# A Fourier mixer and a low-rank MLP: unfolded output weights without sums on GpSimd, and q stored by chunks of 256 tokens

## The chip, the cores and the metric

One core of one Trainium2 chip runs the whole program. The metric is the device time of one launch in microseconds (us). "Median" is over the timed runs of one kernel.

Engine names in profile lines: PE is TensorE (matmuls), PEld its weight loads, DVE is VectorE, ACT is ScalarE, POOL is GpSimd. "L425" is a line of that kernel's source; the line numbers of the two kernels differ by a few.

## The reference

```python
def _attn_ref(x):                        # x [8, 3136, 256] f32
    X = np.fft.fft(x, axis=1)
    X = np.fft.fft(X, axis=2)
    return X.real.astype(np.float32)

def _moe_ref(x, U, V, w_ch1, w_ch2):     # U [3136, 32], V [32, 3136], w_ch1 [256, 1024], w_ch2 [1024, 256]
    xt = x.transpose(0, 2, 1)
    h = xt @ U @ V
    u = x + h.transpose(0, 2, 1)
    ch = np.maximum(u @ w_ch1, 0.0) @ w_ch2
    return (u + ch).astype(np.float32)
# out = _moe_ref(_attn_ref(x), ...)      [8, 3136, 256] f32
```

The residual `u` is never built as a tensor: its two terms enter the output's accumulation as matmuls against small tables.

## The kernel before

The batch is worked in four pairs. In the steady part one step is made of two half-steps, and a half-step is one MLP1 unit (TensorE makes `hps`, ScalarE copies half of it to `ab`, VectorE makes two tiles `hT` out of both with `max`) and one MLP2 phase (16 matmuls of `hT` with `W2`, L480, and then the residual's matmuls against the tables `TK`, `Bp` and `R`, L490). In between, TensorE prepares the next pair: stage 1 (`s`, from the folded input `yb`), and then the transform's second stage (`ln`), which ScalarE copies into `q`, the tile that MLP1 and the residual read.

`W2` and `Bp` are folded: the 256 output columns are kept as 128 sums and 128 differences, so `Bp` is only 128 wide, and each output has to be put together again at the end, on GpSimd:

```python
def drain(eng):                                   # eng is nc.gpsimd but for the last chunk
    ...
    nc.scalar.copy(om, po)                        # ScalarE: PSUM -> SBUF
    eng.tensor_tensor(ob[:, 0:n, 0:P], a, om[:, :, 1], op=AL.add)
    eng.tensor_tensor(ob[:, 0:n, P:D], a, om[:, :, 1], op=AL.subtract)
```

The table part of a phase; each `o` is 256 columns, `half` says which 64 rows of the array the matmul uses, and matmuls on the two halves run side by side:

```python
def group(s, o, half):
    r = slice(64 * half, 64 * half + 64)
    if half == 0:
        yield o, VS[0:64, 1 - s, ...], TK[p2][b][:]
    for blk in range(2):
        w, cs = (RR[1 - s][r, blk], slice(0, D)) if half else (Bp[r, blk], slice(blk * P, (blk + 1) * P))
        yield o[:, cs], qs(r, s, blk), w
```

`q` is `[128, 2, 3200]`: two blocks of 128 columns of the model dimension, each with all tokens of the pair. One copy of 512 tokens writes a stretch in both blocks:

```python
o = q[:, :, c0:c0 + 512].rearrange("p k (i j s) -> p s k i j", i=4, s=2)
evac[0](o, ps[0].rearrange("p s (k i j) -> p s k i j", k=2, i=4))
```

VectorE also folds the next pair's input into `yb`, behind GpSimd's own fold into `y`:

```python
def fold_d(yb, src, l0, l1):
    nc.vector.tensor_tensor(o[:, :, 1:128], i[:, :, 1:128], i[:, :, 255:128:-1], op=AL.add)         # L143
    nc.vector.tensor_tensor(o[:, :, 129:256], i[:, :, 1:128], i[:, :, 255:128:-1], op=AL.subtract)  # L144
    nc.vector.tensor_copy(o[:, :, 0:129:128], i[:, :, 0:129:128])                                   # L145
```

## Time and profile before

| | before |
|---|---|
| time, median of 2 | 542.0 us (541.67 to 542.32) |
| span of the profiled run, mean granted TensorE clock | 543.4 us, 0.946 |
| TensorE from 45 us to the end | 425.2 us busy, 73.2 us idle |
| listed waits there: for q / for hT / for yb | 27.1 / 27.8 / 8.3 us |
| GpSimd busy | 271.4 us |
| the three instructions of the fold into yb, L143 / L144 / L145, mean of 24 | 1446 / 900 / 395 ns |

How to read it: time has to be looked for in TensorE's idle 73 us, and in what of its busy time is spent at the lower clock. The last two rows are not bounds by themselves.

### The profile page before, as it was taken

Reading aid. Unit: us, or ns where it says so; the run is one execution under the profiler, and the core shown is the slowest. Engines: PE = TensorE matmul, PEld = TensorE weight load, DVE = VectorE, ACT = ScalarE, POOL = GpSimd, SP = SyncE. Lnnn points to the kernel's source line nnn. Section 1 sums busy time; section 2 is a strip of 40 time slices with the busy share of each in tenths; the row PEclk is TensorE's granted clock in tenths of the full one; section 3 lists DMA queues with packets and bytes.
Section 4 is the critical chain, followed back from the end, with each engine's and each line's share of the span. In section 5 each row is a group of like instructions: output and inputs, shape, how many; then the busy total and the mean of one; then the engine's idle time right before and its main releaser. Section 6 shows DMA issues by size and latency. Waiting matters only on the chain.

```text
span 543.4 us, 18834 instructions
## 1 busy us (share of the span) xinstructions
PE 455.5 (84%) x8161; PEld 377.4 (69%) x8161; DVE 358.1 (66%) x613; ACT 291.5 (54%) x487; POOL 271.4 (50%) x372
## 2 busy tenths in 40 slices
PE   4886869897999789878888797987889889999996
PEld 2655757676778568757776576766667767888895
DVE  7645688766785456886786367686786355666673
ACT  4774544465644655654643655555454556656552
POOL 7358556467733446756552346574742313333341
PEclk9686998799999998999999999998899989999999
DMA  9436374348418434444515744454322911212122
GB/s 171 124 98 106 90 205 112 103 139 201 152 61 163 160 106 152 134 148 139 163 62 133 158 139 117 140 171 155 117 98 80 181 50 50 72 62 79 61 80 89
DMA packets 58339, 65.50 MB, mean 121 GB/s; under 512 B 11188, under 2 KB 51086, under 8 KB 58094
## 3 DMA queue, kind: packets, MB, share of 16 engines
q1 hardware_dynamic: 48048, 43.48, 27.9%
q0 software_dynamic: 7232, 14.30, 11.8%
q10 hardware_dynamic: 2976, 6.51, 3.2%
q8 instruction: 64, 1.05, 0.8%
q14 instruction: 19, 0.16, 0.1%
HBM read 34.62 MB, written 32.19 MB: 123 GB/s over the span
## 4 chain that ended last, share of the span: by engine, by line
PE 54%; DVE 26%; ACT 11%; issue 4%; DMA 2%; POOL 2%; ACTq 1%; DVEq 0%; POOLq 0%
PE ops L480 22%; PE hps L423 12%; DVE hT L441 7%; DVE hT L438 7%; PE hps L432 6%; PE ops L490 5%; ACT q L82 5%; DVE yb L143 4%; ACT ab L435 3%; DVE g L85 3%; DVE yb L144 2%; PE ln L355 2%; DMA w_f<-in_moe_w_ch_dram 1%; PE te L304 1%; PE teps L332 1%
## 5 line engine op out<-in xcount | busy, mean ns | idle before, releaser
L438 DVE SCALAR_TENSOR_TENSOR hT<-ab,hps 128x512 bf16<-128x512 bf16 x200 | 136.8, 684 | 167.1 <-ACT ab L435 164.8
L480 PE MATMUL ops<-W,hT 64*128 64x256 bf16 x3072 | 214.8, 277 | 13.0 <-DVE hT L441 8.5
L522 POOL TENSOR_TENSOR ob<-om 128x256 f32<-128x256 f32 (+1 forms) x97 | 71.5, 738 | 234.6 <-ACT om L521 225.4
L480 PEld LDWEIGHTS <-hT 64*128 64x128 bf16 x3072 | 158.4, 96 | 38.6 <-DVE hT L441 16.7
L435 ACT CAST ab<-hps 128x512 bf16<-128x512 f32 x200 | 117.1, 589 | 120.9 <-PE hps L432 115.1
L423 PE MATMUL hps<-q,W1p 64*128 64x256 bf16 (+1 forms) x1248 | 132.1, 276 | 41.7 <-ACT q L82 27.4
L441 DVE TENSOR_TENSOR hT<-hps,ab 128x512 bf16<-128x512 f32 x192 | 131.1, 683 | 0.0
L423 PEld LDWEIGHTS <-W1p 64*128 64x128 bf16 x1248 | 72.7, 97 | 58.9 <-issue 34.5
L423 PE MATMUL hps<-q,W1z 64*128 64x256 bf16 (+1 forms) x416 | 104.3, 276 | 0.0
L432 PE MATMUL hps<-VZ,TE 33*128 33x256 bf16 (+1 forms) x896 | 82.7, 267 | 0.6 <-ACT TE L82 0.6
L521 ACT COPY om<-ops 128x512 f32<-128x512 f32 (+1 forms) x97 | 56.4, 581 | 33.2 <-ACT q L82 10.1
L523 POOL TENSOR_TENSOR ob<-om 128x256 f32<-128x256 f32 (+1 forms) x97 | 73.6, 759 | 0.0
L153 POOL TENSOR_TENSOR y<-xa,xb 98x510 f32<-98x510 f32 (+1 forms) x48 | 58.1, 1229 | 2.4 <-DVE yb L145 2.4
L490 PE MATMUL ops<-TK,VS 64*128 64x256 f16 x192 | 52.8, 275 | 0.5 <-ACT TK L82 0.5
L432 PEld LDWEIGHTS <-TE 33*128 33x128 bf16 x896 | 44.7, 98 | 7.1 <-issue 1.6
L423 PEld LDWEIGHTS <-W1z 64*128 64x128 bf16 x416 | 40.3, 97 | 0.8 <-issue 0.4
L82 ACT CAST q<-ln 128x1024 bf16<-128x1024 f32 (+2 forms) x32 | 32.4, 1025 | 12.4 <-PE ln L355 11.9
L490 PEld LDWEIGHTS <-qr 64*128 64x128 bf16 x384 | 36.9, 96 | 2.4 <-issue 0.4
L490 PEld LDWEIGHTS <-q 64*128 64x128 bf16 x384 | 36.8, 96 | 2.4 <-issue 0.3
L490 PE MATMUL ops<-R,qr 64*128 64x256 f16 x192 | 38.0, 279 | 0.0
L82 ACT CAST z<-s 128x1024 bf16<-128x1024 f32 (+1 forms) x24 | 23.0, 959 | 27.6 <-PE s L196 25.8
L490 PE MATMUL ops<-R,q 64*128 64x256 f16 x192 | 36.6, 271 | 0.0
(186 smaller groups left out, 492.3 us busy)
## 6 DMA issues: line engine op xcount, KB each, us to landing
out_dram<-ob SPq DMA_DIRECT2D x192, 128.0 KB
xa<-in_x_dram SPq DMA_DIRECT2D x24, 392.0 KB
zturn<-z ACTq DMA_DIRECT2D x9, 512.0 KB
g<-zturn SPq DMA_DIRECT2D x6, 416.0 KB
g<-zturn SPq DMA_DIRECT2D x6, 384.0 KB
X<-in_x_dram POOLq DMA_DIRECT2D x4, 384.0 KB, 7.7
X<-in_x_dram POOLq DMA_DIRECT2D x2, 744.0 KB, 7.2
zturn<-z ACTq DMA_DIRECT2D x3, 448.0 KB
```

What stands on the lines that cost most here:

```text
L82: nc.scalar.copy(o, i)
L153: nc.gpsimd.tensor_tensor(ck.y[:, l0:l1, 1:256], ck.xa[:, l0:l1, 1:256], rb[:, l0:l1, 255:0:-1], op=AL.add)
L423: nc.tensor.matmul(o[s], lt, q[64 * s:64 * s + 64, blk, c0:c0 + w], start=(i == 0 and blk == 0), stop=True, skip_group_check=True)
L432: nc.tensor.matmul(ps[:, s, i * w + a:i * w + a + n], TE[ch.p % 2][b][64 * s:64 * s + 33, ja], VZ[64 * s:64 * s + 33, b, v:v + n], start=F ...
L435: nc.scalar.copy(ab[:], ps[:, 1])
L438: nc.vector.scalar_tensor_tensor(h[:, 1], b, -1.0, a, op0=AL.mult, op1=AL.max)
L441: nc.vector.tensor_tensor(flip[0][:, :, ::-1], flip[1], flip[2], op=AL.max)
L480: mm = nc.tensor.matmul(op, ch.h[rows[half], s, j, t * P:(t + 1) * P], W2[rows[half], j, :], start=(ha == 0 and j == 0), stop=False, skip_ ...
L490: last = nc.tensor.matmul(*g[k], start=False, stop=(k == len(g) - 1), skip_group_check=True)
L521: nc.scalar.copy(om, po)
L522: eng.tensor_tensor(ob[:, 0:n, 0:P], a, om[:, :, 1], op=AL.add)
L523: eng.tensor_tensor(ob[:, 0:n, P:D], a, om[:, :, 1], op=AL.subtract)
```

## The change

Its intent: outputs that need no sums (GpSimd is left to the input folds), a layout of `q` in which a copy touches only its own chunk, and a shorter front. The products with `Bp` become twice as wide in exchange. The core of the diff (cut; the rest follows from it):

```diff
-    Bp = cpool.tile([P, 2, P], FP16)
+    Bp = cpool.tile([P, 2, D], FP16)
...
-            pr.q = qpool[pr.p % 2].tile([P, 2, 3200], BF16, tag="q", name="q")
+            pr.q = qpool[pr.p % 2].tile([P, 6400], BF16, tag="q", name="q")
...
-        o = q[:, :, c0:c0 + 512].rearrange("p k (i j s) -> p s k i j", i=4, s=2)
+        a = 2 * (b * 1536 + 512 * c)
+        o = q[:, a:a + 1024].rearrange("p (c s) -> p c s", s=2)
...
-            evac[0](o, ps[0].rearrange("p s (k i j) -> p s k i j", k=2, i=4))
+            evac[0](o, ps.rearrange("p s c -> p c s"))
...
-            if half == 0:
-                yield o, VS[0:64, 1 - s, v + t * P:v + t * P + P], TK[p2][b][:]
+            if half != s:
+                yield o, VS[r, v + t * P:v + t * P + P], TK[p2][b][r]
             for blk in range(2):
-                w, cs = (RR[1 - s][r, blk], slice(0, D)) if half else (Bp[r, blk], slice(blk * P, (blk + 1) * P))
-                yield o[:, cs], qs(r, s, blk), w
+                yield o, qs(r, s, blk), (RR[1 - s] if half else Bp)[r, blk]
...
-            om = opool.tile([P, 2, 2, P], FP32, tag="om", bufs=3, name="om")[:, 0:n]
... (two branches for eng)
-            eng.tensor_tensor(ob[:, 0:n, 0:P], a, om[:, :, 1], op=AL.add)
-            eng.tensor_tensor(ob[:, 0:n, P:D], a, om[:, :, 1], op=AL.subtract)
+            nc.scalar.copy(ob[:, 0:n], st.ps[:, 0:n, 0:D])
...
-    nc.sync.dma_start(out=w2_f, in_=moe_w_ch2.rearrange("(t p) (s d) -> p t s d", p=P, s=2))
+    nc.gpsimd.dma_start(out=W2[:], in_=moe_w_ch2.rearrange("(t p) d -> p t d", p=P))
... (w2_fold on GpSimd, the memsets and copies of R, and the factor 0.5 in W1 go;
     the loads of the second batch move up behind those of the first)
```

## The prediction

> **What bounds the kernel now.** I read four views in this order: the page's busy shares and chain, the table of work by stretches, TensorE's waits from 45 us on (before that the front builds tables), and the timeline at the longest waits.
>
> The page says that TensorE (PE) is the bound, but not alone:
>
> ```profile
> PE 455.5 (84%) x8161; PEld 377.4 (69%) x8161; DVE 358.1 (66%) x613; ACT 291.5 (54%) x487; POOL 271.4 (50%) x372
> PE 54%; DVE 26%; ACT 11%; issue 4%; DMA 2%; POOL 2%; ACTq 1%; DVEq 0%; POOLq 0%
> ```
>
> The second line is the chain that ended last: 26% of it is VectorE (DVE) and 11% ScalarE (ACT), so TensorE is regularly held up. By stretches, TensorE is busy 425.2 us of the 498 us from 45 to 543; 72.8 us are idle, and its waits there say why (what waited, for what: us in total, times, longest):
>
> ```profile
> PE hps L423 <- ACT q L82: 27.1, 17, 2.3
> PE hps L423 <- DVE hT L441: 12.7, 20, 1.0
> PE ops L480 <- DVE hT L441: 8.5, 15, 3.8
> PE s L196 <- DVE yb L145: 8.3, 7, 2.4
> PE tps L243 <- DVE hT L441: 4.1, 1, 4.1
> ```
>
> The first row is the first MLP matmul waiting for ScalarE's copy of q; the rest are waits for VectorE. Where nothing is in the way (465 to 468 us), the half-steps (one MLP1 unit, one MLP2 phase) start every 1.75 us, which is pure TensorE.
>
> The q wait in the timeline (start, us, what, and in brackets the idle time before):
>
> ```profile
> 217.22 1.31 ACT L82 CAST q<-ln 128x1024 bf16<-128x1024 f32 x1 [0.74 <-PE ln L355]
> ...
> 218.58 0.38 PE L423 MATMUL hps<-q,W1p 64*128 64x256 bf16 x3 [1.34 <-ACT q L82]
> ```
>
> The L355 matmuls and their copy make q for a later chunk. Yet the chunk already under way stops: its two block-0 matmuls run at 216.96, its block-1 matmuls wait until the copy ends at 218.53. In the order of the built program, with its waits, 18 MLP1 units carry this second wait, always on the third matmul. The tile is [128, 2, 3200]; a copy that writes columns c0 to c0+512 of both blocks spans everything between, block 1 of the earlier columns included. It is a false dependency of the layout.
>
> The VectorE waits:
>
> ```profile
> 237.25 4.13 DVE L143 TENSOR_TENSOR yb<-y 98x508 bf16<-98x508 f32 x1
> ...
> 238.35 2.48 POOL L153 TENSOR_TENSOR y<-xa,xb 98x510 f32<-98x510 f32 x2
> ...
> 242.14 0.62 PE L196 MATMUL s<-yb,F 98*128 98x258 bf16 x4 [2.38 <-DVE yb L145]
> ```
>
> At the shortest such an addition takes some 0.68 us; here 4.13 us, ending after GpSimd (POOL) has done two output sums (L522, L523) and two y folds. Over 21 of them the mean is 1523 ns.
>
> **What the Trainium skill says.** "SBUF — State Buffer", Who interferes with whom: VectorE and GpSimd share a port pair as an exclusive lock; a VectorE instruction with two SBUF inputs is fully blocked by a GpSimd one that reads SBUF, one with a single SBUF input is not. The trace agrees: hT at L438 (one input in PSUM) stays at 671 to 690 ns over 200 instances, L143 goes from 547 to 4133. "TensorE: Matmul & The Clock Gate", Part 1: after an idle window of about 3.4 us the array runs at half clock until it has been busy for a window. The trace agrees: after the 4.1 us wait before 78.43, sixteen L480 matmuls take 1.92 us at 80.88, but 1.05 us at 88.98. "DMA: Bandwidth & Descriptors", SWDGE vs HWDGE vs iDMA: a cast in a transfer needs GpSimd's queue; this explains why W2 moves there. No load here tells what a cast costs beside a plain load.
>
> **The change, part by part.**
>
> (1) q by chunks of 256 tokens. A copy now writes 1024 adjacent elements. In the order of the changed program all 18 second waits are gone; the copy is first waited for by the unit that reuses its PSUM bank, one half-step later. After the end of the L355 matmuls TensorE does one unit (0.66) and one phase (1.12): 1.78 us. The copy begins some 0.2 us after them, so it has time. It also gets shorter: it writes every second bf16 and takes 1302 ns for 128x1024, while the z copy of the same size, written without gaps, takes 1012. Of 27.1 us I count 23, as ScalarE is sometimes still busy when the L355 matmuls end.
>
> (2) Outputs without sums. ScalarE copies PSUM once, as before (588 ns for 128x512), now straight to the output tile; 97 pairs on GpSimd go (71.5 + 73.6 = 145.1 us of its 271.4). That is not on the path by itself: the 225 us that GpSimd waits for om show it. Its worth is the lock. If VectorE is left alone, L143 falls from 1523 to 680 (21 x 0.84 = 17.7 us), L144 from 876 to 680 (4.1), L145 from 402 to 180 (4.7), and the 32 g copies of pair 0 from 16.5 us to 32 x 0.27 = 8.6 (7.9): 34.4 us of VectorE time. The waits that it caused are 12.7 + 8.3 + 4.1, L480's 8.5 less the 3.8 of (4), and 2.5 of s for hT: 32.3 us. The y folds remain (58 us) and VectorE still has about 2.74 us of hT work per 3.5 us step, so I count two thirds: 21.
>
> (3) Matmuls. An unfolded Bp is 256 wide instead of 128. Before, a phase is three slots on the half arrays: 256|256, 128|256, 128 alone, about 267 ns. Now the two TK products share one phase: three slots of 107 ns, then two: 320 + 213 = 533 ns per pair of phases as before. Zero.
>
> (4) Front. At 42.57 ScalarE copies R after waiting 2.13 us for GpSimd's R memset, queued behind W2's fold and the X loads; 0.90 us of copies follow, and the first L480 starts at 46.62 after 3.77 us idle. These copies leave the front: 3.0 us. W2's cast load is issued about where the plain one was (24.65); the first use is at 39.58, so it is hidden, and so is the earlier load of X.
>
> (5) Clock. By stretches the granted clock is 0.84 from 45 to 100 us and 0.96 to 0.98 afterwards: some 46 us at half rate, up to 23 us lost. Those after 46.6, 78 and 242 follow waits that should go or shrink. I count 8 (an estimate).
>
> (6) Tail. The last om copy and VectorE sums become one copy: 1.
>
> Small additions: eight more TK copies (0.37 us each on ScalarE), not on the path.
>
> Sum: 23 + 21 + 3 + 8 + 1 = 56; 542 - 56 = 486 us.
>
> **The rivals.** A: VectorE takes over the freed time. The q wait lets VectorE catch up; without it, the same hT would be waited for a step later. For it: L423 already waits 20 times for hT. Against it: even in the pairs with loads VectorE is busy 85 of 128 us, part of that blocked. It would leave half of (1) and (2): about 508 us. B: the y folds keep the lock. Freed of the sums, GpSimd runs them whenever their data are there, and if that is just when VectorE does the fold before, L143 stays long. The 4.13 us at 237.25 lie mostly under L153, so this is real; it would take 10 to 15 us from (2) and (5), about 498. C: outputs hold up ScalarE, which now waits itself for a free output tile. Four tiles at one per 3.5 us give 14 us, so I give it little: at most 5 us. D: everything goes as it should and the clock stays full: TensorE's busy time less its half-clock excess, plus little idle: about 472.
>
> **Range and chances.** The middle is 486. D gives the low end, 472; rival A gives the high one, 508. A result within 2% (above 531) would need the q wait to come back in full elsewhere and the lock to stay: 4%. Slower: 1%, for an unseen stall. Faster by over 2%: 95%.
>
> **What would show each step.** (1) L423's wait for q under 4 us in total, the 128x1024 q copy near 1.02 us. (2) GpSimd near 125 us busy, L143's mean under 1.0 us (over 1.2: rival B), waits on hT and yb under 15 us in total (over 25: rival A). (3) L480 and L490 per phase unchanged: half-steps still 1.75 us apart where nothing waits. (4) First L480 near 43.6 us; a wait of the W1-W2 product for the W2 load would prove me wrong. (5) Mean clock from 0.946 to 0.96 or more. (6) ScalarE waits for output transfers would show rival C.

## More of the kernel before

In 40 equal slices of the span, this is the busy share of TensorE and of GpSimd in tenths:

```profile
PE   4886869897999789878888797987889889999996
...
POOL 7358556467733446756552346574742313333341
```

GpSimd is at work in every slice. TensorE's row falls to 7 and 8 in the middle, where the pairs with loads are, and stays at 8 and 9 at the end, where nothing is loaded or folded.

## The result, and the profile after

The changed kernel takes **501.0 us** (median of 2, 500.2 to 501.87) against 542.0, and its result is right. The ratio is 0.924 (95% interval 0.917 to 0.932): ratios are the mean time of one kernel's fast runs over that of the other's of the same rounds, so not quite the ratio of the medians. Executions over 1.5% slower than the fastest of the same kernel are left out of the means. On another chip, used for the last four runs, the kernel before took 535.6 us and the changed one 500.9, a ratio of 0.938. So the gain is 35 to 41 us, and below it is counted on the first chip.

The page after, busy shares and the chain that ended last, and the same two rows of slices:

```profile
PE 451.9 (90%) x8161; PEld 364.4 (73%) x8161; DVE 322.5 (64%) x606; ACT 285.6 (57%) x492; POOL 121.7 (24%) x174
...
PE   3877859999899899999999889999999889999996
...
POOL 8492370623400142333300052324100000000000
...
PE 54%; DVE 24%; ACT 11%; issue 5%; ACTq 2%; POOL 2%; DMA 1%; SPq 0%; POOLq 0%; DVEq 0%
```

GpSimd's 271.4 us are now 121.7 and its row has gaps. TensorE's row has nines in the middle. But the chain still runs a quarter of its way through VectorE: what TensorE waits for has become less, and is still of the same sort.

TensorE's waits from 45 to 500 us (what waited, for what: us in total, times, longest):

```profile
PE hps L425 <- DVE hT L443: 8.3, 12, 1.1
PE tps L243 <- DVE hT L443: 6.2, 3, 5.6
PE ops L480 <- DVE hT L443: 4.4, 16, 0.4
PE ops L480 <- ACTq L492: 3.2, 7, 0.8
PE ops L480 <- DVE hT L440: 2.0, 6, 0.5
```

No wait for q is in the list, and none for yb. The waits for hT are 21.1 us, with 0.2 us of a line that is not shown. From 45 us to the end TensorE is idle 33.3 us (73.2 before), and busy 421.8 us (425.2 before). The busy time is made of two changes that go against each other. The clock records of the traces have 44.5 us at half clock in that stretch before, with 40.2 us of matmuls in them, and 15.2 us after, with 10.1. Half of the difference, 15.0 us, is what the clock gave back, and the matmuls themselves, counted at full clock, grew from 405.1 to 416.7 us (both are estimates from these figures, of one trace each, that count work at half clock as taking twice as long: the prediction's sixteen L480 matmuls take 1.92 us there and 1.05 otherwise).

The instances of the fold into yb (shortest/median/longest in ns), first of the kernel before, then of the changed one:

```profile
L143 DVE TENSOR_TENSOR yb<-y x24: 547/1272/4133, 96.2 to 411.5; 98x508 bf16<-98x508 f32 x21, 98x381 bf16<-98x381 f32 x3
```

```profile
L143 DVE TENSOR_TENSOR yb<-y x24: 546/678/832, 88.9 to 371.3; 98x508 bf16<-98x508 f32 x21, 98x381 bf16<-98x381 f32 x3
```

The shortest is the same, the long ones are gone.

One thing went the other way. This is the table part of a phase before, at a place without waits (start, us; the line of L423 is the next unit's first matmul):

```profile
466.19 0.27 PE L490 MATMUL ops<-TK,VS 64*128 64x256 f16 x1
466.19 0.27 PE L490 MATMUL ops<-R,qr 64*128 64x256 f16 x1
466.30 0.22 PE L490 MATMUL ops<-Bp,q 64*128 64x128 f16 x1
466.30 0.27 PE L490 MATMUL ops<-R,qr 64*128 64x256 f16 x1
466.35 0.22 PE L490 MATMUL ops<-Bp,q 64*128 64x128 f16 x1
466.41 0.27 PE L423 MATMUL hps<-q,W1p 64*128 64x256 bf16 x1
```

And this is the first phase of a pair of phases after:

```profile
444.04 0.38 PE L490 MATMUL ops<-TK,VS 64*128 64x256 f16 x2
444.15 0.27 PE L490 MATMUL ops<-Bp,q 64*128 64x256 f16 x1
444.26 0.27 PE L490 MATMUL ops<-R,qr 64*128 64x256 f16 x1
444.26 0.27 PE L490 MATMUL ops<-Bp,q 64*128 64x256 f16 x1
444.37 0.27 PE L490 MATMUL ops<-R,qr 64*128 64x256 f16 x1
444.37 0.27 PE L425 MATMUL hps<-q,W1p 64*128 64x256 bf16 x1
```

Before, from 466.19 to 466.41 pass 0.22 us: two narrow `Bp` matmuls run one after the other on one half, 0.05 us apart, beside one `R` of 256 columns on the other half, and that makes two slots of 0.11 us. After, three slots, 0.33 us. The median from the first table matmul to the next unit is 221 ns over the 192 phases before; after, it is 327 ns over 96 of them and 219 over the other 96. That is 106 ns x 96 = 10.2 us more of matmul time.

### The profile page after: what moved, and what is told of

It reads as the page before. It is cut to its first block, busy times and chain, and to the rows that moved or that the text cites. A ratio compares the mean times of both kernels' runs of the same rounds, so it can differ in the third digit from the quotient of the medians.

```text
span 500.1 us, 18587 instructions
## 1 busy us (share of the span) xinstructions
PE 451.9 (90%) x8161; PEld 364.4 (73%) x8161; DVE 322.5 (64%) x606; ACT 285.6 (57%) x492; POOL 121.7 (24%) x174
## 3 DMA queue, kind: packets, MB, share of 16 engines
q8 instruction: 64, 1.05, 0.9%
## 4 chain that ended last, share of the span: by engine, by line
PE 54%; DVE 24%; ACT 11%; issue 5%; ACTq 2%; POOL 2%; DMA 1%; SPq 0%; POOLq 0%; DVEq 0%
PE ops L480 23%; PE hps L425 11%; DVE hT L440 9%; DVE hT L443 8%; PE ops L490 7%; PE hps L434 6%; ACT ab L437 5%; ACT q L82 2%; DVE g L85 2%; PE te L304 1%; PE s L196 1%; DMA xa<-in_x_dram 1%; ACT z L82 1%; ACTq L380 1%; PE teps L331 1%
## 5 line engine op out<-in xcount | busy, mean ns | idle before, releaser
L440 DVE SCALAR_TENSOR_TENSOR hT<-ab,hps 128x512 bf16<-128x512 bf16 x200 | 136.9, 685 | 159.5 <-ACT ab L437 158.9
L480 PE MATMUL ops<-W,hT 64*128 64x256 bf16 x3072 | 210.0, 271 | 12.6 <-DVE hT L443 4.6
L480 PEld LDWEIGHTS <-hT 64*128 64x128 bf16 x3072 | 150.0, 94 | 44.7 <-DVE hT L443 17.2
L425 PE MATMUL hps<-q,W1p 64*128 64x256 bf16 (+1 forms) x1248 | 123.8, 267 | 9.7 <-DVE hT L443 8.3
L153 POOL TENSOR_TENSOR y<-xa,xb 98x510 f32<-98x510 f32 (+1 forms) x48 | 58.1, 1229 | 207.3 <-DMA xa<-in_x_dram 104.3
L425 PE MATMUL hps<-q,W1z 64*128 64x256 bf16 (+1 forms) x416 | 99.4, 268 | 0.0
L434 PE MATMUL hps<-VZ,TE 33*128 33x256 bf16 (+1 forms) x896 | 80.0, 260 | 0.8 <-ACT TE L82 0.5
L508 ACT COPY ob<-ops 128x512 f32<-128x512 f32 (+1 forms) x100 | 57.9, 579 | 33.2 <-ACT q L82 8.9
L490 PE MATMUL ops<-Bp,qr 64*128 64x256 f16 x192 | 36.8, 272 | 0.0
L490 PE MATMUL ops<-Bp,q 64*128 64x256 f16 x192 | 36.5, 269 | 0.0
L82 ACT CAST q<-ln 128x1024 bf16<-128x1024 f32 (+2 forms) x32 | 25.8, 819 | 7.7 <-PE ln L354 7.7
L82 ACT COPY qr<-q 128x512 bf16<-128x512 bf16 x48 | 29.9, 624 | 0.1
```

Source lines behind the costliest of these rows:

```text
L82: nc.scalar.copy(o, i)
L153: nc.gpsimd.tensor_tensor(ck.y[:, l0:l1, 1:256], ck.xa[:, l0:l1, 1:256], rb[:, l0:l1, 255:0:-1], op=AL.add)
L425: nc.tensor.matmul(o[s], lt, q[64 * s:64 * s + 64, blk], start=(i == 0 and blk == 0), stop=True, skip_group_check=True)
L434: nc.tensor.matmul(ps[:, s, i * w + a:i * w + a + n], TE[ch.p % 2][b][64 * s:64 * s + 33, ja], VZ[64 * s:64 * s + 33, b, v:v + n], start=F ...
L440: nc.vector.scalar_tensor_tensor(h[:, 1], b, -1.0, a, op0=AL.mult, op1=AL.max)
L480: mm = nc.tensor.matmul(op, ch.h[rows[half], s, j, t * P:(t + 1) * P], W2[rows[half], j, :], start=(ha == 0 and j == 0), stop=False, skip_ ...
```

## The experiments

All twelve runs gave the reference's result, but for three that are wrong, as is said there; times are medians of 4 runs each, those of the kernel before of its fast runs in the same rounds. The first eight ran on the first chip, the last four on the other. What the first chip's eight say together, as a table of the two parts that gain (with sums on GpSimd or without, old or new layout of q):

| | old layout of q | new layout of q |
|---|---|---|
| sums on GpSimd, rest as before | 541.8 (before) | 526.3 (q_alone) |
| no sums, rest as before | 512.3 (no_sums) | not run |
| sums-like work on GpSimd, rest changed | not run | 530.0 (pool_tt) |
| no sums, rest changed | 515.5 (q_back) | 501.0 (changed) |

### The layout of q, alone and taken back

`q_alone` is the kernel before with those lines of the diff that concern `q` (tile, copy, and the slices of its readers); `q_back` is the changed kernel without them:

```diff
-            pr.q = qpool[pr.p % 2].tile([P, 6400], BF16, tag="q", name="q")
+            pr.q = qpool[pr.p % 2].tile([P, 2, 3200], BF16, tag="q", name="q")
... (q_back; lines_out and the slices of q follow; q_alone is the reverse, in the kernel before)
```

> The kernel before with the new layout of q alone; everything else as before, a right result. Theory (the waits of the matmuls for the copy of q are a false dependency through the shared tile, and the gain of the whole change is a sum of separate parts): the 27.1 us of waits for q at L351 go, the q copy falls from 1302 to about 1015 ns, the folds on VectorE stay as slow as before (first yb tensor_tensor near 1.5 us in the mean), the waits for hT and yb stay; time 518 to 526 us. Rival (the waits were only a place where TensorE waited for VectorE and ScalarE, which are late anyway, so they pass on to hT): time above 532 us, waits for hT up by more than 15 us.

> The changed kernel with the old layout of q, the rest changed; a right result. In the kernel before, the new layout alone took 16 us off (542 to 526), where its waits were 27.1 us, and the waits for hT grew by 10. Theory (about half of each wait for q covers time in which VectorE is late in any case; without the sums VectorE is less late, so the same layout is worth as much or more here): waits for q at L425 of 20 to 27 us are back, time 514 to 520 us. Rival (with 3 slots in phase 0 TensorE hides the waits): time under 508 us.

`q_alone` took 526.3 us, 15.5 less than before (541.8) and 0.3 us outside the theory's range. Its waits for q are down to 0.4 us, but those for hT rose from 27.8 to 37.4 us, where the theory had them stay. The mean of L143 fell to 1164 ns, where 1.5 us was expected; no run here says why. `q_back` took 515.5 us, 14.5 more than the changed kernel. Its three largest waits:

```profile
PE hps L422 <- ACT q L82: 24.9, 19, 2.2
PE tps L243 <- DVE hT L440: 5.6, 1, 5.6
PE hps L422 <- DVE hT L440: 5.2, 8, 1.0
```

The waits for q are 24.9 us, and those for hT 12.6 in all (21.1 in the changed kernel). So the layout takes 24.9 us of waits away, and 8.5 us of them come back as waits for hT; 16.4 us of the listed waits and 14.5 us of the time are what it is worth. In both surroundings it is about the same.

### Is it the dependency, or the faster copy?

The new layout does two things: it takes the false dependency away, and it makes the copy shorter (1302 to 1013 ns for 128x1024). `slow_q` gives ScalarE the saved time back as work:

```diff
             evac[0](o, ps.rearrange("p s c -> p c s"))
+            sq = apool.tile([P, 156], BF16, tag="sq", bufs=2, name="sq")
+            evac[0](sq[:], ps[:, 0, 0:156])
```

> The changed kernel with a ScalarE copy of 156 elements a row behind each copy of q, about 290 ns, the time that the chunk layout took off the q copy; the result goes nowhere, outputs right. Theory (the layout's gain of 14.5 us lies in the false dependency between chunks, not in the faster copy): time within 2 us of the changed kernel, no waits for q. Rival (ScalarE's time is part of the bound, so the shorter copy is the larger part of the gain): 4 us or more slower, with the waits for hT or ab up by that.

```profile
L82 ACT CAST sq<-ln 128x156 bf16<-128x156 f32 x23 | 6.8, 298 | 0.0
```

The 23 extra copies took 298 ns each, as meant, and the time was 499.7 us, against 500.9 for the changed kernel (the run `after_again`) in the same rounds. So the time that ScalarE saves is worth nothing that can be seen, and the gain is the dependency. One thing this run leaves out: its extra copy stands behind the copy of q, so q itself is still there 0.29 us earlier than with the old copy. No run undoes that; by the prediction's own sum (0.2 + 1.3 us until q is there, 1.78 us of other work for TensorE) it should not be waited for either.

> The changed kernel as it is, on the same chip and in the same rounds as the three next ones, so that small differences can be read: 499 to 503 us, half-steps alternating between 1.75 and 1.86 us.

It took 500.9 us (499.65 to 503.51), so the changed kernel is the same on both chips.

### The sums, taken away alone and put back

`no_sums` is the kernel before, with the drain of the changed one (a wrong result: the sums and differences go out as they are). `pool_tt` is the changed kernel with GpSimd kept as busy as before by sums that nobody reads:

```diff
             nc.scalar.copy(ob[:, 0:n], st.ps[:, 0:n, 0:D])
+            dm = opool.tile([P, 2, 2, P], FP32, tag="dm", bufs=3, name="dm")[:, 0:n]
+            nc.gpsimd.tensor_tensor(dm[:, :, 0], ob[:, 0:n, 0:P], ob[:, 0:n, P:D], op=AL.add)
+            nc.gpsimd.tensor_tensor(dm[:, :, 1], ob[:, 0:n, 0:P], ob[:, 0:n, P:D], op=AL.subtract)
```

> The kernel before with its drain as one ScalarE copy and no GpSimd sums, everything else as before; a wrong result on purpose. Theory (the sums on GpSimd hold up VectorE): the mean of the first fold into yb falls from 1.5 us to about 0.69 us, the waits for hT and yb fall by about 20 us, the waits for q stay at about 27 us or fall to 20 at most; time 515 to 526 us. Rival (the sums held up nothing on the way to the end, the whole gain of the change is in q): time above 534 us.

> The changed kernel with two GpSimd tensor_tensor of 128x256 put back behind each drain, the size of the old sums; their result goes nowhere, nothing waits for them, the outputs stay right. Theory (what the sums cost was the time that VectorE's own instructions were held up beside them): the first fold into yb (L143) goes from 0.68 us back to above 1.2 us in the mean, hT (L440, L443) stays at 0.68, waits for hT and yb rise by over 15 us, time 518 to 530 us. Rival (the sums cost because the outputs waited for them, or because ScalarE had two tiles to serve): time within 5 us of 501, L143 below 0.9 us.

`no_sums` took 512.3 us, 29.5 less than before and better than the theory's range; the waits for q stayed (22.3 us), L143 fell to 666 ns in the mean, and the waits for hT and yb fell by 20.9 us, from 36.1 to 15.2. `pool_tt` took 530.0 us, 29.0 more than the changed kernel, and its result is right. No output waits for the extra sums (only ScalarE does, for its output tile: twice, 1.1 us in all), which rules out the rival that the outputs themselves were late. What is late is VectorE: the mean of L143 is 1188 ns, a little under the 1.2 us expected. The instances of L143 in `pool_tt`, then its timeline at one of them, first VectorE, then GpSimd:

```profile
L143 DVE TENSOR_TENSOR yb<-y x24: 546/1180/2399, 90.4 to 397.1; 98x508 bf16<-98x508 f32 x21, 98x381 bf16<-98x381 f32 x3
```

```profile
132.07 2.40 DVE L143 TENSOR_TENSOR yb<-y 98x508 bf16<-98x508 f32 x1
134.40 1.21 DVE L144 TENSOR_TENSOR yb<-y 98x508 bf16<-98x508 f32 x1
135.52 0.17 DVE L145 CAST yb<-y 98x8 bf16<-98x8 f32 x1
```

```profile
130.60 2.49 POOL L153 TENSOR_TENSOR y<-xa,xb 98x510 f32<-98x510 f32 x2
133.04 0.21 POOL L154 TENSOR_TENSOR y<-xa,xb 98x4 f32<-98x4 f32 x1
133.20 0.73 POOL L510 TENSOR_TENSOR dm<-ob 128x256 f32<-128x256 f32 x1
133.88 1.17 POOL L511 TENSOR_TENSOR dm<-ob 128x256 f32<-128x256 f32 x1
```

L143 has its data, for the profile lists no wait before it. Alone it needs 0.68 us. Here it lasts until 134.47, that is until 0.54 us after L510 has ended: it got no turn beside L153, L154 and L510. L511 in turn lasts 1.17 us where L510 takes 0.73, so it waited for L143, and L144 ends 0.56 us after L511. Of the 48 additions and subtractions of the fold, the 42 with GpSimd work beside them took 1098 ns in the mean, the 6 without took 680. This agrees with the Trainium skill, "SBUF — State Buffer", section Who interferes with whom: a VectorE instruction with two inputs in SBUF and a GpSimd instruction that reads SBUF share a port pair, which one of them holds for the whole instruction. hT, which has one input in PSUM, stayed at 683 ns.

Added up over the folds and the copies into g, VectorE's time in `pool_tt` is 32.4 us above that of the changed kernel, and the whole kernel is 29 us longer. For TensorE, from 45 us on, that is 21.1 us more idle time (54.4 against 33.3) and 7.2 us more busy time (429.0 against 421.8), with 27.4 us at half clock against 15.2. `no_sums` shows the same two parts against the kernel before: 20.3 us less idle and 13.6 us less busy, with 20.8 us at half clock against 44.5.

### The wider Bp

`narrow_bp` makes the `Bp` matmuls in the phases 128 wide again; `narrow_tk` also puts one `TK` product into each phase, as before. Both give wrong results.

```diff
-                yield o, qs(r, s, blk), (RR[1 - s] if half else Bp)[r, blk]
+                w, cs = (RR[1 - s][r, blk], slice(0, D)) if half else (Bp[r, blk, blk * P:(blk + 1) * P], slice(blk * P, (blk + 1) * P))
+                yield o[:, cs], qs(r, s, blk), w
```

```diff
-            if half != s:
+            if half == 0:        # narrow_tk only
```

> The changed kernel with the Bp matmuls of a phase 128 wide again (two of them fill one slot of 256); the TK products stay both in phase 0; a wrong result on purpose. Theory (a phase's table matmuls take the longer of the two halves' column sums): phase 0 has 512 columns on the half with Bp and 768 on the half with R, so it stays at 3 slots, 327 ns, and the time stays within 2 us of the changed kernel's 501. Rival (what costs in phase 0 is the width of Bp itself): 2 slots, half-steps of 1.75 us, time near 491 us.

> The same with one TK product per phase on the half of the narrow Bp, as in the kernel before; a wrong result on purpose. Theory (3 slots of 256 columns in phase 0 are the step in which the gain of the change was given back): all phases at 2 slots, L490 at about 220 ns in each phase, undisturbed half-steps of 1.75 us everywhere where they alternated between 1.75 and 1.86, time 490 to 494 us. Rival (TensorE is not the bound, so a shorter phase turns into waits for hT): time above 498 us and the waits for hT up by about 8 us.

`narrow_bp` took 500.2 us: no gain, as the theory has it, since the half with `TK` and two `R` is as long as it was. But the other half does not wait for it. In its timeline the next unit's matmul is under way before the last `R`, which stands ahead of it in the program:

```profile
442.42 0.27 PE L491 MATMUL ops<-R,qr 64*128 64x256 f16 x1
442.43 0.27 PE L425 MATMUL hps<-q,W1p 64*128 64x256 bf16 x1
442.53 0.27 PE L491 MATMUL ops<-R,qr 64*128 64x256 f16 x1
```

This agrees with the Trainium skill, "TensorEngine Tiling (Array Packing)", section Key Properties, that different tiles of the array work independently.

`narrow_tk` brings back the median of 221 ns, and the undisturbed half-steps are 1.75 us again (62 of them, where the changed kernel has 25 at 1.75 and 42 at 1.86 or 1.87). Yet it took 498.1 us, 2.9 less than the changed kernel and 2.1 less than `narrow_bp` in the same rounds. The theory asked for 490 to 494, and the rival was nearer the mark in time: TensorE's busy time from 45 us on fell by 7.4 us, and its idle time rose by 4.3. But of these only 2.1 us are waits for hT (23.2 against 21.1), not the 8 that the rival asked for. The wider `Bp` costs 10.2 us of matmul time and 3 us of the kernel's.

### The front

`front_back` puts the memsets and ScalarE copies of `R` back into the first step, the second batch's loads behind the front, and all sums of the V rows into step 0. (The plain load of `W2` and its fold are not put back. So the 2.13 us for which ScalarE waited for the memset of `R`, queued behind that fold, are not back either: here the copies of `R` start at 38.78 us without a listed wait.)

> The changed kernel with the front as before: the GpSimd memsets and four ScalarE copies of the residual tables, the loads of the second batch behind the last step of the front, and all GpSimd sums of the V rows in step 0; a right result. Theory (the earlier loads and the shorter front are a small part of the gain): first L480 at 46 to 47 us instead of 43.5, half clock again between 45 and 55 us, time 503 to 508 us. Rival (the front is hidden behind later waits): within 1.5 us of 501.

It took 501.8 us, 0.8 more than the changed kernel. Its first L480 starts at 43.0 us, after a wait of 1.60 us, and the changed kernel's at 43.5 after 0.83; but the granted clock up to 45 us was 1.00 in this run and 0.89 in the other, so the starts can't be compared. (`pool_tt`, with the changed front and that clock also at 1.00, starts at 41.8.) The rival holds: these parts are worth about 1 us. What `W2`'s cast in the load is worth by itself was not run.

### What is left in the first pair

The longest wait of the changed kernel is 5.6 us at 75 us. VectorE and GpSimd just before it:

```profile
66.52 2.89 DVE L542 TENSOR_SCALAR F<-ang,mb 98x384 f16<-98x384 f32 x2 [0.68 <-issue]
69.34 4.38 DVE L85 COPY g<-zt 32x400 bf16<-32x400 bf16 x8
```

```profile
67.05 1.83 POOL L888 MEMSET UZ<- 128x2048 f32 x1
69.55 2.50 POOL L153 TENSOR_TENSOR y<-xa,xb 98x510 f32<-98x510 f32 x2 [0.67 <-ACT R L82]
```

Eight copies into g take 2.13 us where GpSimd is idle, and 4.38 here; the two instructions that make the table F take 0.75 us where nothing is beside them (in `late_fold`), and 2.89 beside a GpSimd memset, 2.57 of them the first. The skill's section named above says so of VectorE's copies, casts and tensor_scalar in their two-port modes. `late_f` makes F two steps later and clears UZ six steps later:

```diff
-            at[5].append(lambda: (..., v_copy(0, NK1, False), rest[0]()))
+            at[5].append(lambda: (..., v_copy(0, NK1, False)))
-            at[7].append(lambda: (v_copy(17, NK1, None), late_tables(), copy_dve(...)))
-            at[12].append(load_uz)
+            at[7].append(lambda: (v_copy(17, NK1, None), rest[0](), copy_dve(...)))
+            at[13].append(late_tables)
+            at[16].append(load_uz)
```

> The changed kernel with the stage-1 table F made two steps later and the GpSimd memset of UZ six steps later, so that neither lies beside the copies into g that TensorE waits for at 75 us; a right result. Theory (F and the memset are what delays hT there): the 5.6 us wait at L243 goes to under 2 us, and the half clock after it (72 to 79 us) with it, time 494 to 497 us. Rival (the copies into g alone keep VectorE late, or the wait moves to the next turned step): time within 2 us of 501.

It took 495.6 us (494.44 to 496.0) with a right result, 5.4 less than the changed kernel. The waits at L243 for hT fell from 6.2 to 1.0 us, and the granted clock from 45 to 100 us rose from 0.94 to 0.97. This version beats both kernels.

### Is VectorE the second bound?

If so, moving the fold into yb from VectorE to the idle GpSimd should help further. Both stand on `late_f`: `late_half` moves the subtraction, `late_fold` the whole fold of y.

```diff
-    def fold_d(yb, src, l0, l1):
+    def fold_d(yb, src, l0, l1, e=nc.vector):
...                       # e.tensor_tensor for nc.vector.tensor_tensor: the subtraction, or all three
-        fold_d(yb, ck.y, 0, 3 if ck.c == 7 else 4)
+        fold_d(yb, ck.y, 0, 3 if ck.c == 7 else 4, nc.gpsimd)
```

> The kernel with F and UZ later (495.6 us), and one of the two tensor_tensor of the fold into yb, the subtraction, on GpSimd instead of VectorE. Theory (VectorE is the second bound, behind the waits for hT of about 15 us that are left; 16 us of its time go to an idle engine): time 489 to 494 us. Rival (GpSimd's tensor_tensor now holds up VectorE's addition of the same fold, as the sums did): 495 us or more, L143 mean above 0.9 us.

> The same with the whole fold into yb of a chunk on GpSimd, so that VectorE has hT and little else in the steady part: 36 us leave VectorE. hT has shown the same 0.68 us beside GpSimd work, so nothing on VectorE should be held up. Theory (VectorE is the second bound): waits for hT at L425 and L480 fall from 14 to under 5 us, time 486 to 492 us. Rival (stage 1 now waits for GpSimd, or TensorE alone is the bound): waits for yb at L196 above 5 us, or time within 2 us of 495.6.

`late_half` took 493.2 us (median of its three fast runs; the fourth, 499.8, was slow) on the second chip, where `late_f` was not run. That is in the theory's range, and the mean of L143 was 711 ns and not the 0.9 us of the rival; but it can't be told from `late_f`. `late_fold` took 509.4 us, far worse. Its longest wait and what VectorE did then:

```profile
PE teps L343 <- DVE g L85: 12.0, 1, 12.0
```

```profile
83.90 15.20 DVE L85 COPY g<-zt 32x400 bf16<-32x400 bf16 x8
```

From 83.7 to 98.9 us GpSimd ran two folds of y and three of yb with hardly a gap, and eight copies that need 2.13 us took 15.20. Two of the eight took 5.85 and 5.87 us, and they ended at 92.68 and 99.10 us, where GpSimd's last fold before a gather (L108) ended at 92.75 and 99.16. That reads as the lock again, with VectorE as the one that loses. And where no such copies are, from 100 to 400 us, little was gained: the waits for hT there are 9.5 us, against 11.9 in `late_f`, though VectorE had 25.5 us less to do there (167.0 against 192.5). So my theory fell: VectorE's load is not what these waits come from. What they come from instead (I would look at the way from `hps` by ScalarE's `ab` to the second hT: 0.59 + 0.68 + 0.68 = 1.95 us, in half-steps of 1.75 to 1.86) no run here shows. It would fit that VectorE's idle time before the first hT (L440) in the changed kernel ended with `ab` for 158.9 of 159.5 us, but that alone does not show it.

## Why the prediction was right or wrong

The time, 501.0 us, lies in the range of 472 to 508, but 15 us above the predicted 486. The gain was 41 us and not 56. Step by step:

| step of the prediction | its term, us | measured, us | by |
|---|---|---|---|
| (1) q by chunks | 23 | 14.5 to 15.5 | q_back, q_alone |
| (2) sums leave GpSimd | 21 | 29.0 to 29.5, clock included | pool_tt, no_sums |
| (3) matmuls | 0 | -2.9 | narrow_tk |
| (4) front | 3 | 0.8 (W2's part not run) | front_back |
| (5) clock | 8 | contained in (1) and (2) | see below |
| (6) tail | 1 | 0.5 | the two traces |
| sum | 56 | 41.9 with the first value of each row | gain: 41.0 |

**(1) was right in mechanism and too large.** The false dependency was there, the waits went, and the copy got as short as foreseen (1013 ns). I counted 23 of 27.1 us because I looked only at whether the copy would be in time. Rival A was right for this term: 8.5 us of the 24.9 come back as waits for hT. The prediction had set marks for it, under 15 us of such waits for its own view and over 25 for the rival's; 21.1 lies between them. In us of the kernel's time this is the largest miss of the sum.

**(2) was right in mechanism, and in size too if the clock is kept apart.** L143's mean is 668 ns for all 24, and of 34.4 us of VectorE time that I expected to go, 35.3 did (18.7 + 5.7 + 5.2 in the fold, 5.7 in the copies). I took two thirds of the waits, 21 us, and in `no_sums` the waits for hT and yb fell by 20.9 and TensorE's idle time by 20.3. What the 29 us have beyond that is busy time at half clock, so it belongs to (5). Rival C was small: ScalarE's output copies waited 1.3 us in all for output transfers. Rival B, that the y folds would keep the lock, did not happen in the folds: 46 of their 48 additions and subtractions run with no GpSimd work beside them. It did in pair 0, at the copies into g. Those have a single input in SBUF, as has L145 (395 ns before, 180 after), and the prediction's reading of the skill, that such an instruction is not blocked, left out the page's condition "outside the 2-port perf modes". So the prediction's clause that one with a single SBUF input is not blocked is too wide; it holds for hT, which also reads PSUM.

**(3) is the step whose mechanism failed.** It put a phase of the kernel before at "three slots on the half arrays: 256|256, 128|256, 128 alone, about 267 ns". It is two: the two narrow matmuls fit one behind the other beside one wide one. The trace that I had showed it (221 ns; my 267 was worked out from a pairing and not read). The Trainium skill has the number too: "TensorE: Matmul & The Clock Gate", section Back-to-back issue gap, gives 262 cycles for 256 columns and 134 for 128 at 2.4 GHz, so about 109 and 56 ns (an estimate from the page), and the trace agrees with 0.11 and 0.05 us. So 10.2 us of matmul time came in that I had at zero. That it cost only 3 goes with TensorE's idle time: `narrow_tk` gives 7.4 us of busy time back and loses 4.3 of them as idle time.

**(4)** The first L480 came at 43.5 us as predicted. W2's load was not waited for. But of the parts that I named as its cause, `front_back` shows about 1 us; the wait behind W2's fold was not put back, so what that was worth stays open.

**(5) was right in kind and too small.** The time at half clock from 45 us on fell from 44.5 to 15.2 us, worth some 15 us (the estimate above) where I had 8. Most of it goes with the sums: 20.8 us are left in `no_sums` and 37.5 in `q_alone`, and with one part undone 27.4 come back in `pool_tt` and 19.9 in `q_back`. So the gains that were measured by undoing a part hold its share of the clock already, and a row of its own must not be added to them: (2) and (5) together were put at 29 and measured 29.0 to 29.5. These are single traces; the kernel before had a mean clock of 0.946 in its trace and of 0.949 to 0.968 in its other fast runs, so part of the 15 us may be the run. Seen by TensorE's time from 45 us on, the change took away 39.9 us of idle time and 15.0 us of half clock and added 11.6 us of matmuls; the prediction had the last of these at zero.

**(6)** From the start of the last output's own `R` matmul to the end of the span pass 6.55 us before and 6.03 after.

## What to carry to other kernels

An idle engine is not free: before work goes to GpSimd, look whether VectorE works from SBUF to SBUF at that time, and read the price from the spread of one VectorE group (shortest against mean), not from GpSimd's share. A wait that is taken away is worth what the next wait behind it leaves of it, here some 15 of 25 us, so undo one part at a time before a sum of terms is believed. And count slots of matmuls from the start times in the trace, half by half: halving a width is worth nothing if the other half of the array is the longer one, and a whole slot if it isn't.

## What the Trainium skill lacked or had wrong

- "SBUF — State Buffer", Who interferes with whom: it says that whoever issues first gets the pair and the other blocks, but not how a row of short instructions fares against an engine that issues without a gap. In `late_fold` eight copies of 0.27 us took 15.20 us beside 15 us of GpSimd work, and two of them alone 5.85 and 5.87 us, each through a whole row of GpSimd instructions.
- The same place: that an instruction which only writes (a GpSimd memset) holds up a VectorE tensor_scalar follows from its text on two-port modes, but no cost is given. Here two instructions took 2.89 us instead of 0.75 (`late_fold`).
- "TensorE: Matmul & The Clock Gate", Part 3: it has matmuls start and end strictly in program order. In `narrow_bp` a matmul on the free half starts at 442.43 us, ahead of one on the other half at 442.53 which the source issues before it. How matmuls of unequal width pack on two halves is not told there: 221 ns with two of 128 columns beside one of 256, 327 ns with all of 256.
- "ScalarE: Activation LUTs" gives no cost for writes with gaps: 1302 ns for 128x1024 into every second bf16, 1013 ns without gaps (the order of the reads from PSUM changed with it).
